# Second MLP by seven block products in both layers, with its weights prepared during the first MLP

## The chip, the cores and the metric

The kernel runs on one core of a Trainium2 chip. The metric is the device time of one execution in microseconds, lower is better: before the change 1142.33 us, the median of three runs (1140.93 to 1144.09). Its own trace has a span of 1138.8 us.

## The reference

Local attention over 4 x 8 heads and 768 positions, then two MLPs on the 3072 tokens of 512 features, each with a hidden layer of 2048. Cut to what is computed:

```python
# attention, for each chunk of 32 positions
k_full = concat([mem_k, k[l_start:r_end]])         # 8 memory keys + 16 left + 32 + 8 right
a = softmax(scale * q_c @ k_full.T);  out_c = a @ v_full
x = out.transpose(0, 2, 1, 3).reshape(3072, 512)
# first MLP
h = x @ moe_w_in
x = where(h > 0, h, exp(minimum(h, 0)) - 1) @ moe_w_out
# second MLP
r = maximum(x @ moe2_w_in, 0)
out = (s * (r * r) + b) @ moe2_w_out
```

## The kernel before

Every matrix product of the MLPs is made of three matmuls (mm3, L305 to L309): both operands are split into a high part (rounded to the format that TensorE takes) and a low part (the rest), and high x high, high x low and low x high are summed in a PSUM bank. A split is a copy that writes the high part (hi_copy, on ACT or DVE by the table ENGINES) and a subtraction on DVE for the low part (sub, L177). The weights lie in DRAM as 64-bit words. A load of 512 KB brings 128 x 512 of them (load_w, L120); two ACT operations (L129, L130) and two DVE operations (L134, L137) make one 32-bit number of each pair, and a copy (L143) and a subtraction split it. The 32 raw loads of one MLP's weights so give 32 resident split tiles (pool wp).

Attention comes in 24 units of 128 tokens. A unit has matmuls for the scores (psS, psVS, L212) and for the values (psV, psVS, L271), a softmax on DVE and ACT (L224 to L230), and from unit 6 on 16 transposes on DVE (L251). The result of a unit goes straight into the token tiles xh and xl of the first MLP (to_x).

The first MLP takes eight tiles of 384 tokens in 16 hidden chunks c: step (t, c) has 12 matmuls into psH (h_mm), ACT (L331, L332) and DVE (L333) form g, gh and gl are split off it, and 12 matmuls add it to the four banks acc0 to acc3. The acc matmuls of a step stand two steps behind its psH matmuls (seq[n_ - 2]). Tile 0 is cut in two parts around tile 1 (HF), with its partial sums in DRAM. Attention units for the next tile, and the loads and conversions of weights, are put between the steps (beside, weights_to). At the end of a tile the four banks are copied to big (L369, L371) and stored to y_dram (L372).

The second MLP works likewise on tiles of 384, 384 and 256 tokens: its weights (w2) are loaded and split during the last tile of the first MLP and its own first tiles. Four tiles of 512 tokens follow. In these the first layer takes two chunks and two 256-token blocks at once (h2_pair): seven block products of 256 columns in place of eight (psG), with block sums of the tokens (sums_y, split_blocks) and of the weights. The weight sums are made during the second MLP (make_s), stored to s_dram and loaded again for each pair (load_s). The second layer is a plain product with 512 columns (acc<-w,gh).

The queue of each engine runs in order. The order in a queue is set when the kernel is built: a list scheduler takes the instructions by priority, which follows the program order, and by a model of when their operands are ready; so neighbouring steps are interleaved. All DMAs around the change are issued by SP.

## Time and profile before

| what | value |
|---|---|
| median of three runs | 1142.33 us (1140.93 to 1144.09) |
| span of the profiled execution | 1138.8 us; its own time is not given apart, the three runs lie 2.1 to 5.3 us above the span |
| PE busy | 1124.0 us, 99%, 9262 matmuls |
| DVE busy | 766.8 us, 67%, 1617 instructions |
| ACT busy | 474.5 us, 42%, 891 instructions |
| bytes moved by DMA | 130.43 MB, mean 115 GB/s |

The span runs from the first instruction to the last. Matmul records overlap, since matmuls are pipelined, so the pace of PE is read from the distance between starts, and not from the duration of one. The windows view gives the busy time of each engine in a stretch, with the granted clock of TensorE (1.00 is 2.4 GHz, 0.50 is 1.2 GHz) and the share of the DMA engines in use. In the timeline, "x7" at the end of a row says that seven instructions are drawn as one, and brackets name the idle time before a row and what ended it.

### The profile page before, as it was taken

The page shows a single profiled execution, that of the slowest core. Times are in us where ns is not written, and L with a number is a line of the kernel's source. Part 1 is how long each engine was busy: PE and PEld are TensorE (multiplying, and loading weights), DVE is VectorE, ACT ScalarE, POOL GpSimd, SP SyncE. Part 2 cuts the span into 40 slices and gives each one's busy share as a digit, 9 for nine tenths or more (in the row PEclk, how much of TensorE's full clock was granted, in tenths as well). Part 3 has the DMA queues.
Part 4 walks back from the last instruction along what each step waited for, and adds up shares of the span by engine and source line. Part 5 has one row for each costly group of instructions (what it writes and reads, how often), then busy time and mean ns, then how long its engine had stood idle before and what let it go on. Part 6 is the DMA issues. An engine that isn't in the chain of part 4 may idle for free.

```text
span 1138.8 us, 22472 instructions
## 1 busy us (share of the span) xinstructions
PE 1124.0 (99%) x9262; PEld 1055.8 (93%) x9262; DVE 766.8 (67%) x1617; ACT 474.5 (42%) x891; POOL 0.7 (0%) x6
## 2 busy tenths in 40 slices
...
GB/s 305 388 215 157 1 96 82 94 48 75 47 75 71 71 75 47 47 47 2 210 259 209 135 141 93 93 56 47 166 112 124 136 111 140 120 111 112 122 101 37
DMA packets 73318, 130.43 MB, mean 115 GB/s; under 512 B 6272, under 2 KB 45952, under 8 KB 73216
## 3 DMA queue, kind: packets, MB, share of 16 engines
...
HBM read 106.43 MB, written 22.54 MB: 113 GB/s over the span
## 4 chain that ended last, share of the span: by engine, by line
PE 88%; ACT 7%; DVE 3%; DMA 1%; issue 1%; ACTq 0%
PE acc L307 14%; PE acc L308 14%; PE acc L309 14%; PE psH L307 9%; PE psH L309 9%; PE psH L308 9%; PE psG L309 5%; PE psG L308 5%; PE psG L307 5%; ACT raw L129 2%; PE psVS L271 1%; ACT raw L130 1%; ACT w L143 1%; PE psVS L212 1%; DVE pt L251 1%; PE psV L271 1%
## 5 line engine op out<-in xcount | busy, mean ns | idle before, releaser
L307 PE MATMUL psH<-xh,w 128*128 128x384 f32 (+1 forms) x704 | 236.1, 335 | 2.6 <-ACT pt L173 1.2
L309 PE MATMUL psH<-xh,w 128*128 128x384 f32 (+1 forms) x704 | 233.8, 332 | 0.0
L308 PE MATMUL psH<-xl,w 128*128 128x384 f32 (+1 forms) x704 | 233.4, 332 | 0.2 <-DVE xl L177 0.2
L331 ACT ACTIVATE g<-psH 128x384 f32<-128x384 f32 x128 | 63.0, 492 | 279.1 <-PE psH L309 210.4
L307 PE MATMUL acc<-gh,w 128*128 128x384 f32 x512 | 172.1, 337 | 0.4 <-DVE big L369 0.3
L309 PE MATMUL acc<-gh,w 128*128 128x384 f32 x512 | 171.2, 334 | 0.0
L308 PE MATMUL acc<-gl,w 128*128 128x384 f32 x512 | 171.2, 334 | 0.0
L307 PE MATMUL acc<-w,gh 128*128 128x512 f32 x384 | 150.3, 392 | 0.3 <-ACT big L371 0.3
L308 PE MATMUL acc<-w,gh 128*128 128x512 f32 x384 | 150.5, 392 | 0.0
L309 PE MATMUL acc<-w,gl 128*128 128x512 f32 x384 | 150.1, 391 | 0.0
L307 PEld LDWEIGHTS psH<-xh,w 128*128 128x128 f32 x704 | 133.3, 189 | 8.0 <-DVE g L333 1.6
L333 DVE SCALAR_TENSOR_TENSOR g<-g,psH 128x384 f32<-128x384 f32 x128 | 70.5, 551 | 100.5 <-ACT g L332 99.6
L308 PEld LDWEIGHTS psH<-xl,w 128*128 128x128 f32 x704 | 133.3, 189 | 2.4 <-DVE xl L177 0.4
L309 PEld LDWEIGHTS psH<-xh,w 128*128 128x128 f32 x704 | 133.1, 189 | 0.2
L309 PE MATMUL psG<-xh,w 128*128 128x256 f32 x448 | 126.8, 283 | 0.0
L308 PE MATMUL psG<-xl,w 128*128 128x256 f32 x448 | 126.8, 283 | 0.0
L307 PE MATMUL psG<-xh,w 128*128 128x256 f32 x448 | 126.6, 283 | 0.0
L177 DVE TENSOR_TENSOR gl<-g,gh 128x384 fp32r<-128x384 f32 (+1 forms) x176 | 95.5, 543 | 33.2 <-ACT gh L173 30.7
L307 PEld LDWEIGHTS acc<-gh,w 128*128 128x128 f32 x512 | 96.1, 188 | 1.5 <-DVE big L369 0.6
L308 PEld LDWEIGHTS acc<-gl,w 128*128 128x128 f32 x512 | 96.1, 188 | 0.1
L309 PEld LDWEIGHTS acc<-gh,w 128*128 128x128 f32 x512 | 96.1, 188 | 0.0
L251 DVE STREAM_TRANSPOSE pt<-sm 32x128 f32<-32x128 f32 x288 | 87.2, 303 | 5.0
...
## 6 DMA issues: line engine op xcount, KB each, us to landing
raw<-w SPq DMA_DIRECT2D x64, 512.0 KB, 5.4
w<-s_dram SPq DMA_DIRECT2D x128, 256.0 KB, 3.5
kb<-k SPq DMA_DIRECT2D x24, 512.0 KB, 5.8
v<-v SPq DMA_DIRECT2D x24, 512.0 KB, 4.0
...
```

What stands on the lines that cost most here:

```text
L129: nc.scalar.activation(out=f(high), in_=f(high), func=AF.Copy, scale=2.0 ** -112)
L130: nc.scalar.activation(out=low, in_=low.bitcast(U32), func=AF.Copy, scale=2.0 ** -29 * (1 - 2.0 ** -15), bias=-0.4999)
L143: nc.scalar.activation(out=hi, in_=f(t), func=AF.Copy)
L177: return nc.vector.tensor_tensor(out=lo, in0=src, in1=f(hi), op=ALU.subtract)
L212: mm = nc.tensor.matmul(ps[o, z, r * NCK:(r + 1) * NCK], q[rows, r * U + c * CH:r * U + (c + 1) * CH], kb[rows, r, c * NCK:(c + 1) * NCK], ...
L251: nc.vector.transpose(out=pt[k * CH:(k + 1) * CH, :, rows], in_=sm[rows, :, z, n0:n0 + CH])
L271: nc.tensor.matmul(ps[r % 2 * D:(r % 2 + 1) * D, z, o:o + CH], v[rows, (r * NC + c) * D:(r * NC + c + 1) * D], pt[rows, r, cs], start=True ...
L307: nc.tensor.matmul(o, sa(a[0]), sb(b[0]), start=first, stop=False)
L308: nc.tensor.matmul(o, sa(a[0]), sb(b[1]), start=False, stop=False)
L309: return nc.tensor.matmul(o, sa(a[1]), sb(b[0]), start=False, stop=last)
L331: nc.scalar.activation(out=g[:, :n], in_=ps[:, :n], func=AF.Relu, scale=-1.0)
L333: nc.vector.scalar_tensor_tensor(out=g[:, :n], in0=g[:, :n], scalar=-1.0, in1=ps[:, :n], op0=ALU.add, op1=ALU.max)
```

## The change

The second MLP is written anew; the first keeps its matmuls. Both layers of the second MLP use seven block products, on three tiles of 1024 tokens with 512-token blocks, so all its matmuls have 512 columns. Each product takes one "piece" of weights, 128 x 512 (high and low part of 128 x 256): there are seven pieces for each of 8 chunk pairs and each layer. prepare() makes them out of the raw words in 16 rounds of 10 steps, in tiles 5 to 7 of the first MLP, and stores them to s_dram; the second MLP streams them, 256 KB each, eleven ahead (next_piece). Several products are summed in the same PSUM bank (BANK), and a copy on ACT (aside) saves what a bank holds before the next product is added. load_blocks loads 1024 tokens and forms the seven token blocks: once after the first MLP, and later beside the products 5, 7 and 3 of the second layer. The attention units of tiles 2 to 7 are stored to x_dram and read back as a tile (load_x), and are put into tiles 2 to 4 (TATT = 5) instead of 2 to 6. In ENGINES the high copies of g move to ACT throughout. The loads of s_sb and b_sb stand at the program's start, behind the first kb and q. The output is stored in the layout (128, 4, 3072) and rearranged on the host.

```diff
@@ -27,8 +27,13 @@
 NU = B * UPB
 NP = H // 2
 NU0 = 6
-HF = {1: 6, 2: 8}
+HF = 6
+TATT = 5
 MICRO = 8
+HN, NT2 = 512, 3
+ORDER = (1, 2, 6, 5, 7, 3, 4)
+BANK = {1: 1, 2: 2, 6: 1, 5: 5, 7: 1, 3: 5, 4: 1}
+PIECE = {1: 0, 2: 1, 4: 2, 5: 3, 6: 4, 7: 5, 3: 6}
 NC, NCK = U // CH, LEFT + CH + RIGHT + NMEM
 QC, KC, VC = NP * U, NC * NCK, NP * NC * D
...
     def to_x(u, ps, behind=None):
         t, jj = tile_of[u]
-        if t not in X:
-            X[t] = x_tiles(t if t < 2 else (t + 1) % 2)
-        xh, xl = (x.rearrange("p (i z) n -> p z i n", z=2)[:, :, :, jj * U:(jj + 1) * U] for x in X[t])
         po = ps[:, :, 256:].rearrange("p z (i n) -> p z i n", i=NP // 2)
-        ins = hi_copy("xh", xh, po), sub(xl, po, xh)
+        if t < 2:
+            if t not in X:
+                X[t] = x_tiles(t)
+            xh, xl = (x.rearrange("p (i z) n -> p z i n", z=2)[:, :, :, jj * U:(jj + 1) * U] for x in X[t])
+            ins = hi_copy("xh", xh, po), sub(xl, po, xh)
+        else:
+            xs = xsp.tile([P, KT, U], F32, tag="xs", name="xs")
+            ins = (hi_copy("xh", xs.rearrange("p (i z) n -> p z i n", z=2), po),)
+            nc.sync.dma_start(out=x_dram[:, :, u * U:(u + 1) * U], in_=xs)
         for i in ins if behind else ():
             wait(i, behind)
+    def load_x(t):
+        X[t] = xh, xl = x_tiles((t + 1) % 2)
+        nc.sync.dma_start(out=f(xl), in_=x_dram[:, :, starts[t] * U:(starts[t] + sizes[t]) * U])
+        nc.scalar.activation(out=xh, in_=f(xl), func=AF.Copy)
+        sub(xl, f(xl), xh)
...
-    def mm3(o, a, b, sa, sb, first, last):
-        nc.tensor.matmul(o, sa(a[0]), sb(b[0]), start=first, stop=False)
-        nc.tensor.matmul(o, sa(a[0]), sb(b[1]), start=False, stop=False)
-        return nc.tensor.matmul(o, sa(a[1]), sb(b[0]), start=False, stop=last)
+    def mm3(o, a, b, sa, sb, first, last, again=False):
+        nc.tensor.matmul(o, sa(a[0]), sb(b[0]), start=first, stop=False, skip_group_check=again)
+        nc.tensor.matmul(o, sa(a[0]), sb(b[1]), start=False, stop=False, skip_group_check=again)
+        return nc.tensor.matmul(o, sa(a[1]), sb(b[0]), start=False, stop=last, skip_group_check=again)
...
+    def prepare(layer, i):
+        a, b = (p2["prep"].tile([P, DM], I32, tag="t", name="t") for _ in range(2))
+        for z, t in enumerate((a, b)):
+            raw = p2["prep"].tile([P, DM, 2], I32, tag="raw", name="raw")
+            nc.sync.dma_start(out=raw, in_=w2[2 * i + z, layer].bitcast(I32).rearrange("p (n z) -> p n z", z=2))
+            yield from to_f32(raw, t)
+        a, b = f(a), f(b)
+        (a11, a12), (a21, a22) = ((t[:, :2 * P], t[:, 2 * P:]) for t in (a, b))
+        if layer:
+            a12, a21 = a21, a12
+        sums = p2["prep"].tile([P, 4, 2 * P], F32, tag="s", name="sums", bufs=1)
+        s1, s2, s3, s4 = (sums[:, j] for j in range(4))
+        for o, x, y, op in ((s1, a21, a22, ALU.add), (s2, s1, a11, ALU.subtract), (s3, a11, a21, ALU.subtract),
+                            (s4, a12, s2, ALU.subtract)):
+            nc.vector.tensor_tensor(out=o, in0=x, in1=y, op=op)
+            if o is not s1 and o is not s3:
+                yield
+        left = p2["prep"].tile([P, 4, 2, 2 * P], F32R, tag="o", name="left")
+        two, one_, at = (b, a11, 1) if layer else (a, a22, 0)
+        rest = 0 if layer else 2
+        two = two.rearrange("p (j n) -> p j n", j=2)
+        nc.scalar.activation(out=left[:, at:at + 2, 0], in_=two, func=AF.Copy)
+        nc.scalar.activation(out=left[:, rest, 0], in_=one_, func=AF.Copy)
+        sub(left[:, at:at + 2, 1], two, left[:, at:at + 2, 0])
+        sub(left[:, rest, 1], one_, left[:, rest, 0])
+        nc.sync.dma_start(out=s_dram[layer, i, :, :3], in_=f(left[:, :3]))
+        yield
+        right = p2["prep"].tile([P, 4, 2, 2 * P], F32R, tag="o", name="right")
+        nc.scalar.activation(out=right[:, :, 0], in_=sums, func=AF.Copy)
+        sub(right[:, :, 1], sums, right[:, :, 0])
+        nc.sync.dma_start(out=s_dram[layer, i, :, 3:], in_=f(right))
+        yield
...
+        if c == 0 and t == TATT:
             actx.close()
-            op.append(ctx.enter_context(tc.tile_pool(name="op2", bufs=3)))
-            p2["ys"] = p2["ts"] = ctx.enter_context(tc.tile_pool(name="ysp", bufs=1))
-            p2["s"] = ctx.enter_context(tc.tile_pool(name="sp", bufs=2))
-            load_y(0)
-            nc.sync.dma_start(out=s_sb, in_=s_in.to_broadcast([P, 1]))
-            nc.sync.dma_start(out=b_sb, in_=b_in.to_broadcast([P, 1]))
+            op.append(mctx.enter_context(tc.tile_pool(name="op2", bufs=2)))
+            p2["prep"] = mctx.enter_context(tc.tile_pool(name="prep", bufs=2, reuse_waits="tile"))
+            p2["steps"] = prepare_all()
         if t < 2:
...
+        prepared(t, 2 * c + 1)
         yield
         beside(a0 + total * (2 * k + 2) // (2 * ks), wt[1])
...
+        prepared(t, 2 * c + 2)
+        if c == NF - 4 and 1 <= (t or 1) < NTILE1 - 1 and t != 1:
+            load_x(max(t, 1) + 1)
...
+    def prepared(t, n):
+        want = NPREP * (2 * NF * (t - TATT) + n) // (2 * NF * (NTILE1 - TATT))
+        while t >= TATT and p2["n"] < want:
+            next(p2["steps"])
+            p2["n"] += 1
+    p2["n"], NPREP = 0, 16 * 10
...
+    pctx.close()
+    mctx.close()
+    xcp, yrp, wsp, g2p, evp, ghp, outp = (
+        ctx.enter_context(tc.tile_pool(name=nm, bufs=k, reuse_waits="tile"))
+        for nm, k in (("xcp", 1), ("yrp", 4), ("wsp", 12), ("g2p", 4), ("evp", 5), ("ghp", 3), ("outp", 4)))
+    psp = ctx.enter_context(tc.tile_pool(name="psp", bufs=8, space=PSUM, reuse_waits="tile"))
...
+    pieces = [(0, i, j) for i in range(NF // 2) for j in ORDER] + [(1, i, j) for j in ORDER for i in range(NF // 2)]
+    pieces = pieces * NT2
+    ws, used = [], [0]
+    def next_piece(layer, i, j):
+        while len(ws) < min(used[0] + 11, len(pieces)):
+            lay, ii, jj = pieces[len(ws)]
+            w = wsp.tile([P, 2, 2 * P], F32R, tag="ws", name="ws")
+            nc.sync.dma_start(out=f(w), in_=s_dram[lay, ii, :, PIECE[jj]])
+            ws.append(w)
+        assert pieces[used[0]] == (layer, i, j)
+        used[0] += 1
+        return ws[used[0] - 1]
+    def load_blocks(t):
+        t0 = t * 2 * HN
+        xc = XC[t] = {j: xcp.tile([P, 2, 2, HN], F32R, tag=f"xc{j}", name=f"xc{j}") for j in ORDER}
+        b12 = yrp.tile([P, 2, HN], F32, tag="yr", name="b12")
+        b11, b21, b22 = (f(xc[j][:, 1]) for j in (1, 2, 3))
+        for o, r, z in ((b11, 0, 0), (b12, 0, 1), (b22, 1, 1), (b21, 1, 0)):
+            nc.sync.dma_start(out=o, in_=y_dram[:, 2 * r:2 * r + 2, t0 + z * HN:t0 + (z + 1) * HN])
+        t3, t2, t4 = (yrp.tile([P, 2, HN], F32, tag="yr", name=nm) for nm in ("t3", "t2", "t4"))
+        for o, x, y in ((t3, b22, b12), (b12, b12, b11), (t2, b22, b12), (t4, b21, t2)):
+            nc.vector.tensor_tensor(out=o, in0=x, in1=y, op=ALU.subtract)
+            yield
+        src = {1: b11, 2: b21, 6: t2, 5: b12, 7: t3, 3: b22, 4: t4}
+        for j in ORDER:
+            nc.scalar.activation(out=xc[j][:, 0], in_=src[j], func=AF.Copy)
+            sub(xc[j][:, 1], src[j], xc[j][:, 0])
+            yield
...
+    def aside(ps, nm):
+        o = evp.tile([P, HN], F32, tag="ev", name=nm)
+        nc.scalar.activation(out=o, in_=ps, func=AF.Copy)
+        return o
...
+    def first_layer(t, i, g):
+        xc, ii, acc = XC[t], i % 2, {}
+        for j in ORDER:
+            w = next_piece(0, i, j)
+            if j in (1, 2, 5):
+                acc[j] = bank("psH")
+            o = acc[BANK[j]]
+            for k in range(2):
+                mm3(o, (w[:, 0], w[:, 1]), (xc[j][:, 0], xc[j][:, 1]), lambda a: a[:, k * P:(k + 1) * P],
+                    lambda a: a[:, k], j in (1, 2, 5) and k == 0, k == 1, j not in (1, 2, 5))
+            if j == 1:
+                m1 = aside(o, "m1")
+            elif j == 2:
+                add(g[:, 0, ii], m1, o)
+            elif j == 6:
+                u2 = aside(o, "u2")
+            elif j == 5:
+                p5 = aside(o, "p5")
+            elif j == 7:
+                add(g[:, 2, ii], p5, o)
+            elif j == 3:
+                add(g[:, 1, ii], u2, o)
+        nc.scalar.activation(out=g[:, 3, ii], in_=o, func=AF.Relu)
+        nc.vector.scalar_tensor_tensor(out=g[:, :3, ii], in0=g[:, :3, ii], scalar=0.0, in1=g[:, :3, ii],
+                                       op0=ALU.max, op1=ALU.mult)
+        nc.scalar.activation(out=g[:, 3, ii], in_=g[:, 3, ii], func=AF.Square)
+        nc.scalar.activation(out=g[:, :, ii], in_=g[:, :, ii], func=AF.Identity, scale=s_sb, bias=b_sb)
+        if ii:
+            sub2(g[:, 1], g[:, 2], g[:, 1])
+            add(g[:, 1], g[:, 1], g[:, 0])
...
+    def second_layer(t, gs, beside):
+        keep, acc = {}, {}
+        for j in ORDER:
+            block = {1: 0, 2: 3, 6: 1, 5: 1, 7: 0, 3: 2, 4: 3}[j]
+            if j in (1, 2, 5):
+                acc[j] = [bank("psL") for _ in range(2)]
+            o = acc[BANK[j]]
+            for q, g in enumerate(gs):
+                gh, gl = (ghp.tile([P, 2, HN], F32R, tag=nm, name=nm) for nm in ("g2h", "g2l"))
+                nc.scalar.activation(out=gh, in_=g[:, block], func=AF.Copy)
+                sub(gl, g[:, block], gh)
+                if j == 1:
+                    sub2(g[:, 0], g[:, 1], g[:, 0])
+                elif j == 2:
+                    sub2(g[:, 3], g[:, 3], g[:, 1])
+                elif j == 6:
+                    sub2(g[:, 1], g[:, 2], g[:, 1])
+                for ii in range(2):
+                    w = next_piece(1, 2 * q + ii, j)
+                    for m in range(2):
+                        mm3(o[m], (w[:, 0], w[:, 1]), (gh[:, ii], gl[:, ii]), lambda a: a[:, m * P:(m + 1) * P],
+                            lambda a: a, j in (1, 2, 5) and q == ii == 0, q == 3 and ii == 1,
+                            j not in (1, 2, 5))
+                if j in (5, 7, 3):
+                    next(beside, None)
+            for m in range(2):
+                if j in (1, 6, 5):
+                    keep[j, m] = aside(o[m], "keep")
+                    continue
+                r = outp.tile([P, HN], F32, tag="r", name="r")
+                if j == 2:
+                    add(r, keep[1, m], o[m])
+                    put(r, t, m, 0)
+                elif j == 7:
+                    add(r, keep[5, m], o[m])
...
+    for _ in load_blocks(0):
+        pass
+    for t in range(NT2):
+        gs = [g2p.tile([P, 4, 2, HN], F32, tag="g", name="g2") for _ in range(NF // 4)]
+        for i in range(NF // 2):
+            first_layer(t, i, gs[i // 2])
+        steps2 = load_blocks(t + 1) if t + 1 < NT2 else iter(())
+        second_layer(t, gs, steps2)
+        assert next(steps2, None) is None
...
-    args.append(nc.dram_tensor("out", (NT, DM), F32, kind="ExternalOutput").ap())
+    args.append(nc.dram_tensor("out", (P, KT, NT), F32, kind="ExternalOutput").ap())
     with tile.TileContext(nc) as tc:
         tile_attention_then_two_mlps(tc, *args)
     r = run_bass_kernel_spmd(nc, [arrays], core_ids=[0])
-    return r.results[0]["out"]
+    return np.ascontiguousarray(r.results[0]["out"].transpose(2, 1, 0)).reshape(NT, DM)
```

Three places in the order of instructions follow. The rows give line, operation, and what is written and read; the numbers behind names tell buffers apart. The lines of the changed kernel differ from those before: its L347 and L348 are L331 and L332 before, its L128 and L129 are the raw conversions L129 and L130, its L323 to L325 are L307 to L309, its L177 is L173.

ACT in tile 5 of the first MLP, before: g is formed for one step after another, and sm1 is a unit of attention.

```order
L331 ACTIVATE g_4606<-psH_4593 128x384
L332 ACTIVATE g_4606<-g_4606 128x384
L226 ACTIVATE sm1_101<-sm1_101 128x2x4x64
L331 ACTIVATE g_4639<-psH_4626 128x384
L332 ACTIVATE g_4639<-g_4639 128x384
```

ACT in tile 5, now: raw are the raw words of two weight tiles, left and right the pieces, t and sums what they are made of.

```order
L128 ACTIVATE raw_5969<-raw_5969 128x512
L129 ACTIVATE raw_5969<-raw_5969 128x512
L128 ACTIVATE raw_6008<-raw_6008 128x512
L129 ACTIVATE raw_6008<-raw_6008 128x512
L347 ACTIVATE g_5911<-psH_5898 128x384
L348 ACTIVATE g_5911<-g_5911 128x384
L415 ACTIVATE left_6064<-t_5967 128x2x256
L177 ACTIVATE gh_5915<-g_5911 128x384
L416 ACTIVATE left_6064<-t_5968 128x256
L347 ACTIVATE g_5959<-psH_5946 128x384
L348 ACTIVATE g_5959<-g_5959 128x384
L422 ACTIVATE right_6070<-sums_6047 128x4x256
```

Four conversions and three copies of a preparation now stand in ACT's queue around two g, with the conversions ahead of the first of them.

PE where the first MLP ends, before: acc0 is the first of the last step's four banks, psH_7364 belongs to the second MLP.

```order
L307 MATMUL psH_7364<-xh_6607,w0_1_6907 128x384
L308 MATMUL psH_7364<-xl_6608,w0_1_6907 128x384
L309 MATMUL psH_7364<-xh_6607,w0_1_6907 128x384
L307 MATMUL acc0_6718<-gh_7291,w1_15_1722 128x384
L308 MATMUL acc0_6718<-gl_7292,w1_15_1722 128x384
L309 MATMUL acc0_6718<-gh_7291,w1_15_1722 128x384
```

PE at the same place, now: xc1, xc2 and xc5 are token blocks of load_blocks, ws are pieces.

```order
L324 MATMUL acc3_7078<-gl_7622,w1_15_1727 128x384
L325 MATMUL acc3_7078<-gh_7621,w1_15_1727 128x384
L323 MATMUL psH_7781<-xc1_7722,ws_7759 128x512
L323 MATMUL psH_7792<-xc2_7723,ws_7761 128x512
L323 MATMUL psH_7812<-xc5_7725,ws_7765 128x512
L324 MATMUL psH_7781<-xc1_7722,ws_7759 128x512
```

No matmul of the second MLP stands among the first MLP's any more.

SP at the end of the first MLP, before: raw are words of w2, and the tokens of the second MLP's first tiles (ys) have their loads between them.

```order
L120 DMA raw1_13_7272<-w2 128x1024
L393 DMA ys_8398<-y_dram_84 128x4x256
L120 DMA raw1_14_7362<-w2 128x1024
L372 DMA y_dram_84<-big_7401 128x384
L372 DMA y_dram_84<-big_7404 128x384
L372 DMA y_dram_84<-big_7407 128x384
```

SP at the same place, now: the first four token loads, xc1, b12, xc3 and xc2, go with the last stores of y.

```order
L380 DMA y_dram_84<-big_7676 128x384
L380 DMA y_dram_84<-big_7679 128x384
L611 DMA xc1_7722<-y_dram_84 128x2x512
L380 DMA y_dram_84<-big_7682 128x384
L380 DMA y_dram_84<-big_7685 128x384
L611 DMA b12_7729<-y_dram_84 128x2x512
L611 DMA xc3_7727<-y_dram_84 128x2x512
L611 DMA xc2_7723<-y_dram_84 128x2x512
L596 DMA ws_7759<-s_dram_86 128x512
```

The token loads stand behind the last tile's stores, and the first piece of weights behind them.

## Rows read from the trace of the kernel before

**Rows 1.** The page: busy time of each engine, and the chain that ended last.

```profile
PE 1124.0 (99%) x9262; PEld 1055.8 (93%) x9262; DVE 766.8 (67%) x1617; ACT 474.5 (42%) x891; POOL 0.7 (0%) x6
...
PE 88%; ACT 7%; DVE 3%; DMA 1%; issue 1%; ACTq 0%
```

**Rows 2.** Windows: PE, PEld, DVE, ACT, POOL busy us; clock, DMA share, GB/s.

```profile
560.00:600.00 40.00, 40.00 (x232) 40.00 (x232) 34.73 (x60) 36.56 (x74) 0.00 (x0) 1.00 0.85 278
600.00:620.00 20.00, 19.98 (x114) 19.32 (x113) 19.70 (x36) 20.00 (x42) 0.00 (x0) 1.00 0.64 212
...
900.00:1000.00 100.00, 100.00 (x634) 91.03 (x633) 56.72 (x111) 30.23 (x46) 0.00 (x0) 1.00 0.39 126
```

**Rows 3.** The timeline of PE: start, duration (us), line, operation.

```profile
400.53 0.33 PE L307 MATMUL acc<-gh,w 128*128 128x384 f32 x1
...
402.44 0.33 PE L309 MATMUL acc<-gh,w 128*128 128x384 f32 x1
...
622.84 0.33 PE L307 MATMUL psH<-xh,w 128*128 128x384 f32 x1
...
883.85 0.39 PE L307 MATMUL acc<-w,gh 128*128 128x512 f32 x1
...
887.70 0.39 PE L309 MATMUL acc<-w,gl 128*128 128x512 f32 x1
...
1134.64 0.39 PE L309 MATMUL acc<-w,gl 128*128 128x512 f32 x1
```

**Rows 4.** The timeline of ACT at the end, a copy out of a bank.

```profile
1134.39 0.60 ACT L371 ACTIVATE big<-acc 128x512 f32<-128x512 f32 x1 [0.76 <-PE acc L309]
```

**Rows 5.** Groups by line and form: busy us, mean ns of one, idle before.

```profile
L177 DVE TENSOR_TENSOR gl<-g,gh 128x384 fp32r<-128x384 f32 x160 | 88.7, 555 | 26.9 <-ACT gh L173 24.4
...
L333 DVE SCALAR_TENSOR_TENSOR g<-g,psH 128x384 f32<-128x384 f32 x128 | 70.5, 551 | 100.5 <-ACT g L332 99.6
L332 ACT ACTIVATE g<-g 128x384 f32<-128x384 f32 x128 | 67.6, 528 | 3.3
L331 ACT ACTIVATE g<-psH 128x384 f32<-128x384 f32 x128 | 63.0, 492 | 279.1 <-PE psH L309 210.4 <-DVE gl L177 61.7 <-DVE sm L230 7.0
L129 ACT ACTIVATE raw<-raw 128x512 f32<-128x512 f32 x64 | 44.0, 688 | 9.7 <-DMA raw<-w 9.7
...
L173 ACT ACTIVATE gh<-g 128x384 fp32r<-128x384 f32 x80 | 42.3, 529 | 15.8 <-DVE g L333 14.9
...
L506 ACT ACTIVATE hb<-hb,b_sb,s_sb 128x1024 f32<-128x1024 f32 x32 | 39.8, 1244 | 109.5 <-DVE hb L505 109.5
L505 DVE SCALAR_TENSOR_TENSOR hb<-hb 128x1024 f32<-128x1024 f32 x32 | 39.1, 1223 | 0.9
```

**Rows 6.** The DMA issues, and the raw words' time to landing.

```profile
ys<-y_dram SPq DMA_DIRECT2D x1, 512.0 KB, 3.8
...
DMA to landing us min/median/max: 3.4/5.4/11.4
```

**Rows 7.** The timeline of DVE, two operations in a row.

```profile
599.47 0.68 DVE L137 SCALAR_TENSOR_TENSOR t<-raw,t 128x512 int32<-128x512 int32 x1
600.07 0.69 DVE L134 SCALAR_TENSOR_TENSOR t<-raw 128x512 int32<-128x512 int32 x1
```

**Rows 8.** The windows near the start, columns as in rows 2.

```profile
70.00:75.00 5.00, 3.59 (x71) 3.01 (x71) 4.70 (x14) 4.58 (x10) 0.00 (x0) 1.00 0.31 113
75.00:80.00 5.00, 4.86 (x48) 4.53 (x41) 5.00 (x10) 3.81 (x8) 0.00 (x0) 0.66 0.92 301
85.00:90.00 5.00, 5.00 (x47) 4.66 (x46) 4.71 (x9) 5.00 (x11) 0.00 (x0) 1.00 1.02 416
```

**Rows 9.** The timeline of DVE, a unit's first reduction to its last transposes.

```profile
273.00 0.68 DVE L224 TENSOR_REDUCE nmx<-psVS 128x8 f32<-128x512 f32 x1
...
282.43 2.21 DVE L251 STREAM_TRANSPOSE pt<-sm 32x128 f32<-32x128 f32 x7
```

**Rows 10.** The timeline of SP at the start.

```profile
1.65 0.42 SPq L161 DMA_DIRECT2D kb<-k  x1
```

319 lines of the change are left out of this document (85 added, 234 removed), and 5 rows, old and new, of the table ENGINES.

## Prediction

> **What bounds the kernel now.** I read the page's busy times and chain first: TensorE (PE) is busy 99% of the 1138.8 us span and the chain of waits that ended last is 88% PE, 7% ACT, 3% DVE [rows 1]. So matmul time removed is time won, if what feeds it keeps pace. The windows by stage say where that is doubtful. In the last full stretch before the second MLP (600 to 620 us) ACT is busy 20.00 of 20 us and DVE 19.70 while PE still gets 19.98: two helpers without reserve beside a PE without holes. In the second MLP's main part (900 to 1000) DVE has 56.72 of 100 and ACT 30.23: reserve there [rows 2]. Third, PE's timeline for the pace of matmuls and for the stage's ends: the spacing of starts is 1.91 us over 11 intervals of 384 columns (0.174 each), 3.85 over 17 of 512 (0.2265 each); the first MLP gives way to the second's psH at 622.84, and the last matmul of all starts at 1134.64 [rows 3]. The execution's own time isn't given apart from its span; the median, 1142.33, is 3.5 us above the span, and I work in span and add that 3.5.
>
> **The change, part by part.**
>
> *Second MLP, PE.* From 622.84 to the end of the last matmul (1135.03) are 512.2 us [rows 3]; 24 psH matmuls of the stage stand already between the first MLP's last ones, 24 × 0.174 = 4.2. Before: 516.4. After: per 1024 tokens 8 × 7 × 2 × 3 = 336 for the first layer and 7 × 8 × 2 × 3 = 336 for the second, times three tiles: 2016 of 512 columns, × 0.2265 = 456.6. Gain 59.8, if PE never waits.
>
> *Does it wait in the body?* First layer, one chunk pair: 42 matmuls, 9.5 us of PE. ACT has three copies aside, a Relu and a Square of 512 columns (0.60 each, as the copy of 128x512 out of a bank [rows 4]) and one Identity over 2048 columns, two of the 1.24 us that 1024 take [rows 5]: 5.5. DVE has three adds (0.69 each, as other 512-column operations), one of 1536 columns (1.8, from 1.22 for 1024) and half of two of 1024: 5.1. The shares are fine, but the products share banks: product 6 waits for the copy of product 1, 7 for that of 6, 4 for the add of 7, with one product (1.36 us) between, and in ACT's order the Identity (2.5 us) stands before the next u2 or m1 copy. Following two pairs through I get the Identity from 12.1 to 14.6, u2's copy to 15.2 where PE wants the bank at 14.95. So 0.3 to 0.5 us per two pairs, twelve times. Second layer: 12 matmuls (2.72 us) per group; DVE two operations of 1024 columns, 2.45 by their durations, ACT one of 1.24. It just fits. I take +5 for the body; bounds 0 (all within the cover) and +20 (C below).
>
> *The boundary.* Before, PE goes from acc straight to psH of the other MLP at 622.84, since tokens were loaded and split a tile ahead. After, the first block loads stand on SP behind the last tile's y stores, and nothing of the second MLP runs before them: an uncovered stretch. The copy out of the bank (0.6) and the issue put the first load at about +0.5 us after the last acc matmul, then 3.8 us to landing as the 512 KB load of tokens now takes [rows 6], and the others behind at 512 KB over some 350 GB/s (between 278 at a share of 0.85, so 327 [rows 2], and the 416 of 85 to 90 us [rows 8]), 1.5 apart: the third, which t3 needs, at about +7. DVE then has 11 operations of 1024 columns in one queue: 12.4 if they follow each other at the start-to-start spacing of 512 (0.60, [rows 7], some 1.13 for 1024), 13.5 by durations. Its last two low parts are xc3's and xc4's, out at +19 and +20.5; the 12 matmuls on them end at +23.4. By then PE has done 45 matmuls, 10.2 us. Stall 13.2. After it the clock: a row shows what short holes do to it. From 70 to 75 us PE was busy 3.59 of 5 at a granted clock of 1.00, and the next 5 us had 0.66 [rows 8]: 3.4 us of them at 1.2 GHz, 1.7 us of work lost. Behind the stall as much may be lost, part of it in the shade of DVE. I take +14; bounds 10 (loads land sooner, DVE at spacing) and 20 (all 45 matmuls at half clock as well). The Trainium skill has it in "TensorE: Matmul & The Clock Gate", Part 1, The HAM clock gate: the throttled clock is the default, and activity releases it. The trace agrees, with the 0.66 that follows the holes; by that rule the matmuls that end the stall start at 1.2 GHz and the boundary is 14.9 with the row's 1.7, by a clock that stays up it is 13.2.
>
> *Preparation in tiles 5 to 7.* 16 preparations, each two raw loads of 512 KB, on ACT four conversions of 512 and high copies of 512, 256 and 1024 columns: 3840 columns; on DVE 4864 columns. By 0.69 us per 512 [rows 5] ACT needs 5.2 and DVE, by spacing 0.60 [rows 7], 5.7. In the order ACT has two g between most preparations (11 of 15). With them PE has two steps of 24 matmuls, 8.34 us. ACT adds two g with their high copy, 2 × (0.49 + 0.53 + 0.53) = 3.1 (the last is 0.529 [rows 5]): 8.3 by durations, about 6.7 by spacing. DVE adds 2 × (0.551 + 0.555) by durations or 0.93 each by spacing: 7.6 to 8.7. Tracing one cycle with its waits I get 8.8: 0.5 over PE, 16 times, less some 4 us by which PE's bank buffers and the later g give way. +5; bounds 0 and 20 (1.2 per preparation over 16). What goes: in before, conversion of the same raw weights, 64 operations each, lies in tile 7 and the second MLP's head, with PE at 19.98 of 20.
>
> *DMA.* A preparation moves 2.8 MB (1 in, 1.75 out), in 8.8 us 318 GB/s, beside the 327 to 416 that these stretches reach. In before raw loads land in 3.4 to 11.4 us, median 5.4 [rows 6], and the order gives them about 5.4 to 6.0 of lead. The streaming in the second MLP is one 256-KB piece per 1.36 us, 193 GB/s with 11 ahead: no term.
>
> *Attention squeezed into tiles 2 to 4.* A unit with three g takes DVE from 273.00 to 284.64, 11.6 us [rows 9], in three steps of PE (12.5). In three tiles instead of five the units stand 3 to 4 steps apart; the casts and xl's subtraction leave DVE, the 1536-column split per tile comes. +2; bounds 0 and 8 (0.5 per unit). The high copies of g that move to ACT cost nothing in tiles 2 to 4: 0.53 us of a 4.17 us step, and the acc matmuls stand two steps behind; without that cover it would be some the copy's 0.53 per step.
>
> *Ends.* Two tiny DMAs on SP stand before the second kb and q; an issue takes 0.42 [rows 10]: +0.8 at most 1.2, at least 0 (the load before them is what the first unit waits for). At the end a copy of 512 columns (0.60 [rows 4]) instead of two halves and 256 KB instead of 128: +0.6, 0 to 1. The output's other layout keeps the bytes: no term.
>
> *Sum.* −59.8 + 5 + 14 + 5 + 2 + 0.8 + 0.6 = −32.4: span 1106.4, time 1110.
>
> **Rivals.**
> A, the forecast, 1110. Half of the way to all lower bounds (−17) and a quarter of the way to all upper ones (+43) gives it 1101 to 1121.
> B, all is covered: preparation, attention and body cost nothing, the boundary 10. −59.8 + 10 + 1 = −49: 1094. For it: 600 to 620 us shows ACT and DVE full without harm to PE [rows 2]. Against: before, the two were full for one tile, here for three.
> C, the second layer runs at DVE's and ACT's pace, not PE's: if half of ACT's high copy (0.62 of 1.24) stands uncovered before DVE's 2.45, a group takes 3.07 instead of 2.72. There are 36 groups with block differences (products 1, 2 and 6) and 22 with the next tile's blocks: 58 × 0.35 = 20 in place of the +5, so 1125. For it: two 1024-column operations on DVE per group are 90% of it. Against: three buffers of the split g.
> D, slower than before: raw loads land later than their lead. ACT works in order, and the conversions stand before the next g in it; each us late holds g, then acc, then PE. With 3 us late in 13 of 16 preparations +39 comes on top of the forecast: 1149. It is slower from some 2.5 us late on each. For it: 11.4 us to landing happens in before when loads queue [rows 6], and 318 GB/s is near the lower of the two ceilings. And SP has each pair of raw loads behind the stores of earlier pieces, which wait for DVE's low parts. Against: in 560 to 600 us the same loads at 278 GB/s left PE at 40.00 of 40 [rows 2].
> That the change doesn't do what it says is excluded for the count: PE's list has the 2016.
>
> **How the numbers follow.** A 0.58, B 0.12, C 0.15, D 0.12, others 0.03. What can be told from no change is 0.3%, 3.4 us. A, B and C are all faster: 0.85. D is spread around 1149, with a third of it at or under 1139: same 0.05, slower 0.10. The range leaves out the better half of B and most of D: 1097 to 1136; the likeliest case's own is 1101 to 1121.
>
> **What would show it.** PE's idle in the second MLP: one hole of about 13 us behind the first MLP's last matmul, and then starts 0.2265 apart, with the stage some 476 us from its first matmul's possible start to its end. If the groups of the second layer stand 3.1 apart, C. In tiles 5 to 7 the windows show ACT and DVE above 90% and PE at 97% or more; if PE falls to 85% there and ACT idles before the raw conversions with a DMA as releaser, D. If the hole at the boundary is under 10 or over 20, my reading of DVE's queue there is wrong; the forecast fails as a whole if the three tiles of preparation cost over 25 us.

## The result

The changed kernel takes 1114.66 us, the median of four runs (1113.57 to 1116.7), beside 1142.07 of four runs before: a ratio of 0.9759 with a 95% interval of 0.9744 to 0.9774. That is 27.4 us less. Forecast were 1110 and 32.4 us less, in a range of 1097 to 1136. The profiled span fell by 26.5 us, from 1138.8 to 1112.3; the median of the runs lies 2.4 us above the latter.

The page of the changed kernel, its busy times and the chain that ended last:

```profile
PE 1072.5 (96%) x8206; PEld 965.0 (87%) x8206; DVE 785.8 (71%) x1299; ACT 593.3 (53%) x939; POOL 0.7 (0%) x6
...
PE 75%; DVE 9%; DMA 7%; ACT 5%; issue 2%; SPq 0%; DVEq 0%; ACTq 0%
```

PE is now idle for 39.8 us of its span, where it was idle for 14.8 [rows 1], and the chain holds 7% of DMA and 9% of DVE. The matmuls removed are won, and part of them is given back in waits. The windows show where (columns as in rows 2):

```profile
450.00:500.00 50.00, 48.99 (x283) 48.67 (x282) 45.62 (x87) 40.14 (x76) 0.00 (x0) 1.00 0.88 321
...
620.00:640.00 20.00, 7.69 (x39) 6.65 (x38) 6.04 (x8) 7.22 (x10) 0.00 (x0) 0.72 0.67 233
...
900.00:1000.00 100.00, 100.00 (x439) 81.76 (x439) 63.05 (x62) 46.73 (x54) 0.00 (x0) 1.00 0.73 214
```

Amid the preparation (450 to 500) PE is busy 98% at 321 GB/s; in the body of the second MLP 100%; between the MLPs (620 to 640) it stands still for most of 20 us at a falling clock. PE's own list of waits (time in total, times, longest) gives the causes:

```profile
PE psH L323 <- DMA ws<-s_dram: 11.8, 1, 11.8
PE psP L248 <- DVE sm L234: 3.8, 1, 3.8
PE psS L216 <- DMA q<-q: 2.5, 1, 2.5
PE psV L275 <- ACT pt L177: 2.3, 4, 1.0
PE acc L323 <- ACT big L379: 2.3, 2, 1.3
PE psL L324 <- DVE g2l L181: 1.9, 2, 1.4
```

And the timeline of PE at the boundary and at the end:

```profile
626.06 0.34 PE L325 MATMUL acc<-gh,w 128*128 128x384 f32 x1
638.19 0.76 PE L323 MATMUL psH<-xc,ws 128*128 128x512 f32 x1 [11.79 <-DMA ws<-s_dram]
639.47 0.80 PE L323 MATMUL psH<-xc,ws 128*128 128x512 f32 x1 [0.52 <-ACT xc L618]
640.42 0.80 PE L323 MATMUL psH<-xc,ws 128*128 128x512 f32 x1 [0.15 <-ACT xc L618]
642.10 0.79 PE L324 MATMUL psH<-xc,ws 128*128 128x512 f32 x1 [0.89 <-DVE xc L181]
...
645.25 0.61 PE L325 MATMUL psH<-xc,ws 128*128 128x512 f32 x1
645.68 0.42 PE L323 MATMUL psH<-xc,ws 128*128 128x512 f32 x1
...
1107.99 0.39 PE L325 MATMUL psL<-g2h,ws 128*128 128x512 f32 x1
```

The second MLP's stage runs from 626.23 to 1108.38, 482.2 us, where the 2016 matmuls alone take 456.6. Of the 25.5 us between, 17.1 are the boundary: 12.0 of hole, 3.2 by which the first four matmuls stand too far apart, 1.8 of matmuls at half clock (starts 0.43 apart until 645.68), and 0.1 of a small gap behind them. The other 8.4 are spread over some 460 us. The rest of the loss lies ahead of 626: before the change the same matmuls were done at 622.66 with 24 matmuls of the second MLP among them (4.2 us), so at 618.5; now at 626.06. That is 7.6 us.

The table has the same points of all kernels: when ACT begins to copy bank 0 at the end of tiles 1 and 4 (after tile 4 the changed kernel has no attention left), the starts of the first MLP's last, the second's first and the second's last matmul, the span, and the time of all runs beside those of before. Single traces differ by up to 2.5 us at tile 1 and by up to 4 us between tiles 1 and 4 for the same program part, so differences of a stage are read inside a trace.

| kernel | tile 1 | tile 4 | last of first MLP | first of second | last | span | ratio of the times (95%) |
|---|---|---|---|---|---|---|---|
| before | 144.90 | 410.00 | 622.66 | (622.84) | 1134.64 | 1138.8 | 1 |
| changed | 147.69 | 427.04 | 626.06 | 638.19 | 1107.99 | 1112.3 | 0.9759 (0.9744 to 0.9774) |
| e1_start | 146.81 | 426.71 | 625.02 | 637.25 | 1107.21 | 1111.3 | 0.9731 (0.9713 to 0.9748) |
| e2_big | 148.16 | 429.75 | 625.68 | 636.57 | 1106.34 | 1110.7 | 0.9714 (0.9693 to 0.9734) |
| e3_ahead | 148.06 | 427.28 | 626.22 | 638.50 | 1107.09 | 1111.4 | 0.9755 (0.9738 to 0.9772) |
| e5_prefetch | 147.18 | 430.36 | 630.21 | 633.80 | 1102.92 | 1107.0 | 0.967 (0.9638 to 0.9701) |
| e6_all | 144.09 | 423.65 | 619.66 | 624.03 | 1088.49 | 1092.6 | 0.9608 (0.959 to 0.9627) |
| e7_hold | 148.41 | 428.72 | 628.47 | 639.96 | 1108.76 | 1113.1 | 0.9759 (0.9745 to 0.9774) |
| e8_warm | 149.71 | 430.18 | 629.93 | 641.31 | 1111.65 | 1116.0 | 0.9764 (0.9744 to 0.9785) |
| e9_two | 145.09 | 425.26 | 621.55 | 622.89 | 1089.51 | 1093.6 | 0.9591 (0.9576 to 0.9605) |

### The profile page after: what moved, and what is told of

Read it like the earlier page. It is cut to its first block, busy times and chain, and to the rows that moved or that the text cites. A ratio compares the mean times of both kernels' runs of the same rounds, so it can differ in the third digit from the quotient of the medians.

```text
span 1112.3 us, 20640 instructions
## 1 busy us (share of the span) xinstructions
PE 1072.5 (96%) x8206; PEld 965.0 (87%) x8206; DVE 785.8 (71%) x1299; ACT 593.3 (53%) x939; POOL 0.7 (0%) x6
## 4 chain that ended last, share of the span: by engine, by line
PE 75%; DVE 9%; DMA 7%; ACT 5%; issue 2%; SPq 0%; DVEq 0%; ACTq 0%
PE psH L323 13%; PE psH L324 12%; PE psH L325 12%; PE psL L324 6%; PE psL L325 6%; PE psL L323 6%; PE acc L323 5%; PE acc L325 5%; PE acc L324 5%; DMA xc<-y_dram 2%; DMA raw<-w 2%; PE psVS L275 1%; DVE pt L255 1%; DVE t L132 1%; ACT raw L129 1%
## 5 line engine op out<-in xcount | busy, mean ns | idle before, releaser
L323 PE MATMUL acc<-gh,w 128*128 128x384 f32 x512 | 171.6, 337 | 5.1 <-ACT big L379 2.3
L323 PE MATMUL psH<-xh,w 128*128 128x384 f32 x512 | 174.3, 341 | 0.9 <-DVE g L349 0.6
L324 PE MATMUL psH<-xl,w 128*128 128x384 f32 x512 | 172.6, 337 | 0.2 <-DVE xl L181 0.2
L325 PE MATMUL psH<-xh,w 128*128 128x384 f32 x512 | 172.4, 337 | 0.0
L325 PE MATMUL acc<-gh,w 128*128 128x384 f32 x512 | 171.3, 335 | 0.0
L323 PE MATMUL psH<-xc,ws 128*128 128x512 f32 x336 | 133.6, 402 | 13.4 <-DMA ws<-s_dram 11.8
L679 ACT ACTIVATE g2h<-g 128x1024 fp32r<-128x1024 f32 x84 | 88.9, 1059 | 90.1 <-PE psL L325 89.8
L324 PE MATMUL psL<-g2l,ws 128*128 128x512 f32 x336 | 130.9, 390 | 1.9 <-DVE g2l L181 1.9
L324 PE MATMUL psH<-xc,ws 128*128 128x512 f32 x336 | 131.8, 392 | 0.9 <-DVE xc L181 0.9
L325 PE MATMUL psH<-xc,ws 128*128 128x512 f32 x336 | 131.8, 392 | 0.0
L325 PE MATMUL psL<-g2h,ws 128*128 128x512 f32 x336 | 130.7, 389 | 0.0
L181 DVE TENSOR_TENSOR g2l<-g,g2h 128x1024 fp32r<-128x1024 f32 x84 | 102.2, 1223 | 39.5 <-ACT g2h L679 39.2
L323 PE MATMUL psL<-g2h,ws 128*128 128x512 f32 x336 | 130.1, 389 | 0.0
L347 ACT ACTIVATE g<-psH 128x384 f32<-128x384 f32 x128 | 62.6, 489 | 116.6 <-PE psH L325 77.0
L177 ACT ACTIVATE gh<-g 128x384 fp32r<-128x384 f32 x128 | 67.0, 523 | 87.9 <-DVE g L349 87.1
L323 PEld LDWEIGHTS acc<-gh,w 128*128 128x128 f32 x512 | 95.9, 188 | 7.5 <-ACT big L379 2.9
L323 PEld LDWEIGHTS psH<-xh,w 128*128 128x128 f32 x512 | 96.9, 189 | 3.2 <-DVE g L349 1.2
L325 PEld LDWEIGHTS psH<-xh,w 128*128 128x128 f32 x512 | 97.0, 189 | 0.0
```

The lines of the kernel that those rows point to most:

```text
L177: return nc.scalar.activation(out=hi, in_=src, func=AF.Copy)
L181: return nc.vector.tensor_tensor(out=lo, in0=src, in1=f(hi), op=ALU.subtract)
L323: nc.tensor.matmul(o, sa(a[0]), sb(b[0]), start=first, stop=False, skip_group_check=again)
L324: nc.tensor.matmul(o, sa(a[0]), sb(b[1]), start=False, stop=False, skip_group_check=again)
L325: return nc.tensor.matmul(o, sa(a[1]), sb(b[0]), start=False, stop=last, skip_group_check=again)
L347: nc.scalar.activation(out=g[:, :n], in_=ps[:, :n], func=AF.Relu, scale=-1.0)
```

## The experiments

**e1_start: two tiny loads moved off the start.**

```diff
     set_up()
-    nc.sync.dma_start(out=s_sb, in_=s_in.to_broadcast([P, 1]))
-    nc.sync.dma_start(out=b_sb, in_=b_in.to_broadcast([P, 1]))
...
             p2["steps"] = prepare_all()
+            nc.sync.dma_start(out=s_sb, in_=s_in.to_broadcast([P, 1]))
+            nc.sync.dma_start(out=b_sb, in_=b_in.to_broadcast([P, 1]))
```

> The loads of s_sb and b_sb go back to the start of tile 5; all else as in the changed kernel (span 1112.3 us). Theory: these two DMAs stand on SP before the second kb and q and put each later load back by 1.25 us (the second kb is issued at 2.90, before the change at 1.65), a unit of attention then misses its turn, and the 129th acc matmul comes 3.8 us late (127.30 instead of 123.46). Then that matmul is back at 123.5 to 124.5, and the time falls by 3 to 4 us. Rival: the start lost its time by the units and high copies that the change moves; then the matmul stays near 127 and the time falls by less than 1 us.

SP at the start, first of the changed kernel, then of e1:

```profile
1.65 0.58 SPq L461 DMA_DIRECT2D s_sb<-s  x1
2.27 0.59 SPq L462 DMA_DIRECT2D b_sb<-b  x1
2.90 0.59 SPq L165 DMA_DIRECT2D kb<-k  x1
```

```profile
1.65 0.42 SPq L165 DMA_DIRECT2D kb<-k  x1
```

The second kb is back at 1.65, and the long wait of psP for the softmax is gone. It is 3.8 us in the changed kernel's list above; in e1's it is:

```profile
PE psP L248 <- DVE sm L234: 0.4, 1, 0.4
```

A wait of psP of 3.4 to 3.8 us, at 27 to 29 us, stands in all six traces with the loads at the start and in none of the four without (e1, e6, e9, e10). But the 3.8 us of the expectation at one acc matmul were misread: 123.46 and 127.30 belong to two different matmuls of the same group (the 196th and the 202nd). The 205th starts at 127.10 before the change, at 129.90 now and at 129.02 in e1, so 2.8 us were lost there, and this trace wins back 0.9, there as at tile 1, and not 3 to 4. In the six traces with the loads at the start tile 1 ends at 147.2 to 149.7, mean 148.2; in three without (e1, e6, e9) at 144.1 to 146.8, mean 145.3 (e10 has 145.8). So the cause is right, with 2.9 us on the mean, and one trace alone is too coarse for it. The time of the runs, 1111.25 us, is 3.4 under the changed kernel's, but the two intervals overlap.

**e2_big: more buffers for the copies out of the banks.**

```diff
-                        o = big_tile(n, m == 3 and t >= 2)
+                        o = big_tile(n, m >= 2 and t >= 2)
```

> From tile 2 on the third bank's copy too goes into a spare tile of the weights' staging pool, where only the fourth did. Theory: with the pool op2 of two buffers the copies out of the banks wait for the stores, which is what PE waits for at the ends of tiles 5 and 6 (1.01 and 1.29 us) and what holds SP's third store at the end of tile 7 by 1 us. Then these waits go, and the time falls by 2 to 3.5 us: the preparation itself costs PE nothing. Rival: ACT and DVE are late there because of the preparation's load; then PE's waits for the banks stay and the time changes by less than 1 us.

The windows of e2 in tiles 5 and 6:

```profile
430.00:480.00 50.00, 50.00 (x290) 50.00 (x289) 46.22 (x89) 41.25 (x79) 0.00 (x0) 1.00 0.87 316
480.00:530.00 50.00, 50.00 (x291) 50.00 (x290) 44.22 (x82) 40.01 (x75) 0.00 (x0) 1.00 0.86 316
```

PE is busy all the time with the preparation as it was. From tile 4's end to the first MLP's last matmul it is 195.9 us in place of 199.0, and the hole behind it falls by 1.2. (The boundary as a whole falls by 0.2 only, to 16.9: more matmuls behind the hole are at half clock.) The theory holds: the preparation costs PE nothing, and what it seemed to cost is a pool of two buffers whose third copy waits for a store to land. The time of the runs, 1108.98 us, is 5.7 under the changed kernel's, more than the 2 to 3.5 expected; the trace shows 3.1 in this stage and 1.3 behind it, and what the rest is stays open. In the changed kernel this shows on ACT, behind the last acc matmuls:

```profile
627.35 0.49 ACT L379 ACTIVATE big<-acc 128x384 f32<-128x384 f32 x1 [1.98 <-DMA y_dram<-big]
```

The third bank was full at about 625.5; its copy starts at 627.35, and SP's store behind it holds the token loads that follow, all but the first:

```profile
626.39 0.41 SPq L611 DMA_DIRECT2D xc<-y_dram  x1
627.86 0.80 SPq L380 DMA_DIRECT2D y_dram<-big  x2
628.75 0.43 SPq L611 DMA_DIRECT2D b<-y_dram  x1
```

**e3_ahead: 4 pieces ahead in place of 11 for the first chunk pair.**

```diff
-        while len(ws) < min(used[0] + 11, len(pieces)):
+        while len(ws) < min(used[0] + (4 if used[0] < 7 else 11), len(pieces)):
```

> The first chunk pair loads its weight pieces 4 ahead instead of 11. Theory: behind the first MLP the 13 pieces that SP issues at once share the DMA engines with the token loads, so that the third of these lands 6.8 us after its issue where 512 KB took 3.8 before the change; with 4 pieces it lands in 4.5 to 5, PE's hole of 12.0 us shrinks by 1.5 to 2, and so does the time. Rival: the four loads of 512 KB take this long among themselves; then the hole stays within 0.5 us.

The hole is 12.1 us, as in the changed kernel. This decides nothing: the edit changes the program order of the loads and not when SP may issue them. SP issues 13 pieces in a row at the boundary here too, as it does in the changed kernel from 630.43:

```profile
630.61 14.60 SPq L596 DMA_DIRECT2D ws<-s_dram  x13
```

**e7_hold: the same question, with a wait.**

```diff
-            nc.sync.dma_start(out=f(w), in_=s_dram[lay, ii, :, PIECE[jj]])
+            dma = nc.sync.dma_start(out=f(w), in_=s_dram[lay, ii, :, PIECE[jj]])
+            if 2 <= len(ws) < 11:
+                wait(dma, first_t3[0])
```

> Before, 4 ahead in place of 11 changed nothing in what SP issues at the boundary (13 pieces in 14.6 us both times), so the question is still open. Here the pieces from the third to the eleventh wait, on SP, for the first block subtraction, which needs the third token load; all else as in the changed kernel. Theory: the pieces share the full DMA engines (376 to 398 GB/s from 632 to 636 us) with the token loads; without them the third load lands in 4.5 to 5 us and not 6.8, the first subtraction starts 1.5 to 2.5 us sooner after the last acc matmul than 10.1 us, and the second MLP begins that much sooner. Rival: the four token loads and the stores fill the engines among themselves; then the subtraction starts within 0.5 us of now, and the time is the same or up to 2 us more, since the later pieces come later.

DVE's first block subtraction, in the changed kernel and in e7:

```profile
636.16 1.23 DVE L614 TENSOR_TENSOR t<-xc,b 128x1024 f32<-128x1024 f32 x1 [9.16 <-DMA xc<-y_dram]
```

```profile
637.90 1.22 DVE L616 TENSOR_TENSOR t<-xc,b 128x1024 f32<-128x1024 f32 x1 [8.50 <-DMA xc<-y_dram]
```

Counted from the last acc matmul it starts at +9.4 in place of +10.1; the hole is 11.3 in place of 12.0, and the time is the same (1114.58 us). So 0.7 us is the pieces' share, between the two expectations and nearer to the rival.

**e5_prefetch: tokens loaded and their blocks subtracted before the first MLP ends.**

```diff
+        if t == NTILE1 - 1 and n == 2 * NF - 12:
+            p2["ctx"].close()                       # the preparation's memory
+            p2["yr"] = ctx.enter_context(tc.tile_pool(name="yrp", bufs=4, side="right", reuse_waits="tile"))
...
+            load_first()                            # four loads, t3, b12, t2, t4
...
-    for _ in load_blocks(0):
-        pass
+    for j in ORDER:
+        nc.scalar.activation(out=xc[j][:, 0], in_=p2["src"][j], func=AF.Copy)
+        sub(xc[j][:, 1], p2["src"][j], xc[j][:, 0])
```

> The preparation ends six steps before the first MLP does; its memory then takes the first 1024 tokens, and their loads and the four block subtractions lie beside the last steps of tile 7. Theory: the boundary (17.1 us over matmuls without holes: 12.0 of hole and 5.1 behind it) is the landing of the tokens and DVE's eleven operations in a row. Without the landing and the four subtractions it is the first piece's landing (4 to 5 us after the last acc matmul) and some matmuls at half clock: 5 to 7, and the time falls by 10 to 12 us. Rival: the hole is set by the pieces of weights, whose buffers come free only with the first MLP's last matmuls, and by the throttled clock; then it falls by 5 us or less.

PE behind the first MLP:

```profile
630.21 0.34 PE L325 MATMUL acc<-gh,w 128*128 128x384 f32 x1
633.80 0.47 PE L323 MATMUL psH<-xc,ws 128*128 128x512 f32 x1 [3.25 <-DMA ws<-s_dram]
...
635.30 0.63 PE L325 MATMUL psH<-xc,ws 128*128 128x512 f32 x1
636.47 0.76 PE L323 MATMUL psH<-xc,ws 128*128 128x512 f32 x1 [0.55 <-DMA ws<-s_dram]
...
643.88 0.50 PE L323 MATMUL psH<-xc,ws 128*128 128x512 f32 x1 [0.46 <-ACT u L648]
```

The boundary falls from 17.1 to 8.0 us (3.4 of hole, 0.9 for the second piece, 0.6 for a copy aside, the rest nearly all half clock). That is more than the 5 to 7 of the theory and far from the rival; the time falls by 10.3 us, within the 10 to 12. (The 7.0 in the expectation of e9 below stop short of the matmuls that are still at half clock up to 641.3, and of the copy.) So the landing of the tokens and DVE's subtractions were most of the boundary. What is left of the hole is the landing of the first piece, which now has no token loads ahead of it.

**e8_warm: PE kept at work in the hole.**

```diff
+    wb = bank("warmb")
+    for _ in range(48):
+        nc.tensor.matmul(wb[:, :P], ident, ident, start=True, stop=True)
     for _ in load_blocks(0):
```

> Added: 48 matmuls of a constant 128x128 tile into a spare bank, behind the last acc matmul of the first MLP, so that PE is at work in the hole while tokens and pieces land. Theory: the granted clock (0.50 from 630 to 645 us) falls because PE stands still, and the 13 matmuls with 0.43 between starts instead of 0.227 cost 2.6 us; with PE at work the clock is still 1.00 when the second MLP's matmuls begin, and the boundary falls from 17.1 us by 1.5 to 2.6 (less where DVE's low parts, one each 1.13 us, come too late for the faster matmuls). Rival: DVE's operations set the end of the boundary in any case; then the matmuls have starts 0.227 apart, with waits for DVE between, and the boundary is within 0.7 us of now.

PE's timeline (the 48 matmuls stand in the trace as 96), and the windows of e8 around it:

```profile
630.10 10.88 PE L718 MATMUL warmb<-ident 128*128 128x128 f32 x96
641.31 0.47 PE L323 MATMUL psH<-xc,ws 128*128 128x512 f32 x1 [0.33 <-DMA ws<-s_dram]
...
645.18 0.79 PE L324 MATMUL psH<-xc,ws 128*128 128x512 f32 x1 [1.18 <-DVE xc L181]
645.77 0.63 PE L325 MATMUL psH<-xc,ws 128*128 128x512 f32 x1
646.20 0.63 PE L323 MATMUL psH<-xc,ws 128*128 128x512 f32 x1
```

```profile
635.00:640.00 5.00, 5.00 (x47) 5.00 (x46) 0.77 (x1) 1.47 (x2) 0.00 (x0) 1.00 1.03 374
640.00:645.00 5.00, 2.45 (x12) 1.35 (x11) 4.96 (x5) 4.15 (x5) 0.00 (x0) 0.92 1.05 388
645.00:650.00 5.00, 4.82 (x11) 3.76 (x12) 5.00 (x6) 1.74 (x3) 0.00 (x0) 0.50 0.72 243
```

The clock stays at 1.00 through the hole, and yet is 0.50 from 645 on: between 640 and 645 PE is busy 2.45 of 5 us, since its first matmuls wait for one high copy or low part after the other. The matmuls behind them are 0.43 apart again, and the boundary is 17.3 us; the time is the same (1114.0 us). Neither expectation is met: it is not DVE that sets the end of the stretch (no waits stand there), and keeping PE at work in the hole alone does not help, as the clock falls behind the stutter that follows.

**e6_all and e9_two: the edits together.** e6 has e1, e2 and e5. e9 adds two pieces of weights that are loaded with the tokens, and has one buffer less for the copies aside (evp, 4 in place of 5).

> The three edits together: the loads of s_sb and b_sb at tile 5, the spare tiles for the third bank, and the tokens loaded and their blocks subtracted beside the first MLP's last steps. Alone they gave 1.6 us at the 129th acc matmul (1.2 us between the spans), about 3 us over tiles 5 to 7 and the boundary, and 9 us at the boundary. Theory: they lie in three separate places of one chain of PE, so they add up, less the 1.2 us of the stores' hold that the second and third both take away: 12 to 14 us under the changed kernel's 1114.7, 1101 to 1103. Rival: the matmuls behind them are held by another wait that comes forward (DVE's low parts, the attention's units), then two thirds of it, 1105 to 1107.

> As the three edits together, and with the first two pieces of weights loaded with the tokens, before the first MLP ends (the other pieces have 11 buffers in place of 12, 10 ahead). With the tokens in place the first matmul of the second MLP waited 3.3 us for its piece, and a second wait of 0.6 and 15 matmuls at half clock followed: 7.0 us in all. Theory: only the piece's landing keeps PE; with two pieces there it waits for the first high copy and low part (1.06 and 1.22 us, behind the copies out of the banks), the hole falls to 2 us and with it most of the half clock: 2 to 4 us under the three edits alone. Rival: the blocks' own memory comes free only with the last matmuls and the later pieces land as late as now; then the wait moves from the first to the third piece and 0 to 1.5 us are won.

```diff
+        for j in ORDER[:2]:
+            w = p2["two"].tile([P, 2, 2 * P], F32R, tag="w", name="ws")
+            nc.sync.dma_start(out=f(w), in_=s_dram[0, 0, :, PIECE[j]])
...
-        while len(ws) < min(used[0] + 11, len(pieces)):
+        while len(ws) < min(used[0] + 10, len(pieces)):
```

e6 takes 1095.93 us, 18.7 under the changed kernel, more than the 12 to 14 of the theory. By stages of its trace: 3.6 at the start, 3.0 from tile 4's end to the first MLP's end (196.0 in place of 199.0), and 13.1 in the second MLP's stage (469.1 us from 619.8 to 1088.9, in place of 482.2): the boundary is 5.9 in place of 17.1, and the other 1.9 lie in the body. So no part is lost beside the others, as the theory says. Its sum was too low: e1's own trace had shown little of the start, and the edits together win more at the boundary (11.2) than e5 alone (9.1), where the theory took 1.2 off. PE in e9:

```profile
621.55 0.34 PE L325 MATMUL acc<-gh,w 128*128 128x384 f32 x1
622.89 0.49 PE L323 MATMUL psH<-xc,ws 128*128 128x512 f32 x1 [1.00 <-ACT xc L742]
623.83 0.51 PE L323 MATMUL psH<-xc,ws 128*128 128x512 f32 x1 [0.45 <-ACT xc L742]
```

The hole falls from 4.2 to 1.2 us, with a second one of 0.7, as the theory has it, and the boundary from 5.9 to 3.9, now behind ACT's high copies. That is 2.0 us, the least of the 2 to 4 expected. Only 0.9 of it is left at the end of the stage (468.2 us in place of 469.1), as the body takes 1.1 longer. The times, 1095.6 and 1095.93, don't tell the two kernels apart: a gain from the two pieces is shown at the boundary and not in the time. Both beat the changed kernel and the one before: e9 by 0.9591 (0.9576 to 0.9605).

**e10_alone: the token loads with nothing beside them.** As e6, and the four loads stand later in the program and wait for a late g:

```diff
-            nc.sync.dma_start(out=o, in_=y_dram[:, 2 * r:2 * r + 2, z * HN:(z + 1) * HN])
+            wait(nc.sync.dma_start(out=o, in_=y_dram[:, 2 * r:2 * r + 2, z * HN:(z + 1) * HN]), last_g[0])
```

> As the three edits together, but the four token loads wait for the g of the first MLP's fourteenth chunk in tile 7, some 25 us after the last store of pieces (in the kernel with the three edits that store of 1 MB ran beside them, and they landed in 4.3 to 6.9 us). Only the landing of the four loads is read from it. Theory: four loads of 512 KB in a row slow each other; alone on the DMA engines too the third and fourth land in 5.5 to 6.5 us. Rival: the store slowed them; alone each lands in 3.8 to 4.5 us, as the single load did before the change, and the loss at the boundary beyond the forecast is the y stores' and pieces' traffic.

SP's loads, DVE's first block subtraction, and the windows between:

```profile
610.00 1.91 SPq L576 DMA_DIRECT2D b<-y_dram  x4
```

```profile
616.69 1.23 DVE L579 TENSOR_TENSOR t<-b,b 128x1024 f32<-128x1024 f32 x1 [1.41 <-DMA b<-y_dram]
```

```profile
608.00:610.00 2.00, 2.00 (x13) 2.00 (x12) 0.56 (x1) 1.02 (x2) 0.00 (x0) 1.00 0.00 0
...
612.00:614.00 2.00, 2.00 (x13) 2.00 (x12) 0.42 (x1) 1.02 (x2) 0.00 (x0) 1.00 1.02 393
614.00:616.00 2.00, 2.00 (x14) 2.00 (x13) 0.69 (x2) 0.53 (x1) 0.00 (x0) 1.00 1.05 399
```

The engines are empty before, then full at 393 to 399 GB/s. The third load, issued at 610.94, has landed just before DVE starts at 616.69: 5.7 us, as the theory says, and 6.7 behind the first issue. The fourth took 6.5. In the changed kernel the subtraction starts 636.16 − 626.39 = 9.8 behind the first issue. (The one time taken, 1100.22 us, is no verdict.)

## Why the prediction was right, step by step

- **PE's gain of 59.8 us**: right. The body's matmuls stand 0.227 apart, and 900 to 1000 us has PE at 100.00 of 100.
- **The body, +5**: 8.4. Named ones account for 3.8 (1.5 and 0.7 where a second layer begins and waits for a low part; 1.0 for a copy aside; 0.24, 0.12 and 0.12 at one place in each of the three tiles), the rest are delays of under 0.12 us each. C did not come: DVE's low part waited for ACT's high copy 32 times, 39.2 us in all, but PE waited for it 1.9. These are the rows of the list of waits for this and for D below:

```profile
DVE g2l L181 <- ACT g2h L679: 39.2, 32, 2.0
...
ACT raw L128 <- DMA raw<-w: 4.0, 6, 1.4
```

- **The boundary, +14**: 17.1. The step that failed is "the third, which t3 needs, at about +7": it landed at +10. The 6.5 us that I gave it from the first issue hold for loads that follow each other alone (6.7, e10). But SP did not issue them so: a store whose copy waited for a buffer held the second by some 1.9 us (without that the subtraction starts 1.3 sooner, e2), and the pieces take another 0.7 (e7); the last 1 us is not separated by a run. The y stores are what else stands there: in e2, where SP issues all four of them ahead of the loads, the first load is issued at +1.4 and not at the +0.5 of the forecast. How the loss came about was also otherwise. I had PE work 45 matmuls among DVE's operations and end on DVE's last low parts. In truth nothing ran for 12 us, as the first piece of weights landed as late as the tokens, and the last low part (at 647.64 + 1.22) held nobody. DVE's fifth operation did, the low part that the fourth matmul in PE's order, at 642.10, waits for:

```profile
640.83 1.22 DVE L181 TENSOR_TENSOR xc<-xc 128x1024 fp32r<-128x1024 f32 x1
```

In all six traces with this order (changed, e1, e2, e3, e7, e8) the fourth matmul starts 6.0 us behind the landing of the third token load, whatever moved that landing (by up to 1.4 us). So the third load and five operations of DVE are 15.2 us of the boundary, and the late piece, ahead of three matmuls only, is hidden in them. The half clock cost 1.8, near the 1.7 that I took from rows 8 (but 2.8 to 2.9 in e2 and e8). By the rule from the Trainium skill ("TensorE: Matmul & The Clock Gate", Part 1, The HAM clock gate) the hole leaves the engine throttled, and the trace agrees (0.50 behind it). In e8, with PE at work through the hole, the granted clock fell all the same, behind 5 us in which PE was busy for 2.45. That the hole (12.0) and the boundary came out near the 13 and 14 of the forecast is in part luck.
- **The preparation, +5**: 3.0, and none of it for the reason given. The cycle was near (8.8 worked out; the raw conversions of two preparations on ACT stand 8.6 us apart at first, below, and later 9 us and more), but ACT and DVE at 80 to 92% kept ahead of PE, as rival B had it; the 3.0 are the copies' buffers (e2).

```profile
454.06 0.67 ACT L128 ACTIVATE raw<-raw 128x512 f32<-128x512 f32 x1
...
462.68 0.66 ACT L128 ACTIVATE raw<-raw 128x512 f32<-128x512 f32 x1
```

- **D**: did not come. Raw loads landed as follows, beside 3.4/5.4/11.4 [rows 6]; ACT waited for them 4.0 us in six places and PE never.

```profile
DMA to landing us min/median/max: 3.1/5.8/10.2
```

- **Attention, +2**: 7.6 less 2.8 of start and 3.0 of preparation leaves 1.8. This is a remainder, smaller than what single traces differ by between tiles 1 and 4, so the term is not shown.
- **The start, +0.8**: 2.8 to 2.9. I had priced two issues; in fact each load behind them was issued 1.25 us later, and PE then waited 3.8 us for the softmax of an early unit (0.4 without the two loads, e1).
- **The end, +0.6**: 0.1.

The sum of the measured terms is −59.8 + 8.4 + 17.1 + 3.0 + 1.8 + 2.8 + 0.1 = −26.6, and the spans differ by 26.5. (That it closes proves little, since the attention's term is what the others leave.) Against the forecast the body, the boundary and the start are 8.5 us worse, the preparation, the attention and the end 2.7 better.
